# A new order of all steps in a fused attention and feed-forward kernel on one core

## The chip, the cores and the metric

The kernel runs on one core of one Trainium2 chip. The metric is the device time of one execution in microseconds (us). Engines are named as the profile names them: PE is TensorE, DVE is VectorE, ACT is ScalarE, POOL is GpSimd, and SP is the engine whose queue issues the DMAs.

## What is computed

Per batch and head, k and v (576 rows of 64) are averaged in groups of 8, which leaves 72 rows; softmax attention of the 576 queries against them gives x, and x goes through a layer norm and a feed-forward block with a residual:

```python
k_p = k.reshape(B, H, Sp, pool, D).mean(axis=3)
v_p = v.reshape(B, H, Sp, pool, D).mean(axis=3)
scores = scale * np.matmul(q, k_p.transpose(0, 1, 3, 2))
...
attn = attn / (np.sum(attn, axis=-1, keepdims=True) + 1e-09)
attn_out = np.matmul(attn, v_p)
...
xn = (x - mu) / np.sqrt(var + 1e-06) * g_ln
ch = np.maximum(xn @ w_ch1, 0.0) @ w_ch2
return x + ch
```

There are 8 batches, 8 heads, 512 model columns and 2048 hidden columns, all in float32.

## The kernel before

The 4608 tokens are 36 tiles of 128, taken in 9 chunks of 512. Weights and activations are held as pairs of float16 numbers (a high and a low part), so that a float32 product is three float16 products on PE. From chunk 2 on the products with w1 (L779, step U), and from chunk 3 on those with w2 (L1002, step E), use a scheme with seven products in place of eight, for which sums of weight blocks are formed (steps T and F) and those for w2 are kept in DRAM and streamed back (L977, step D). Chunks 0 and 1 take the direct way: L1067 for w1 (step I) and L1102 for w2 (steps O and P).

At the start everything has to be made ready. The weights are loaded raw (R, L326) and put together in several pieces (C: ACT L337 and L358, POOL L343, DVE L349). The largest element of each weight sets a power of two for the split. For that (M1 for w1, M2 for w2) DVE takes a maximum per partition (L365, L366, L272, L273), PE copies it across (L295) and DVE reduces it again (L304). Only then can S split the weight: ACT writes the high part (L309), DVE the low part (L311). In the same time the first batches of k and v are averaged on PE (K L1218, V L1234), later ones on DVE (L1132, L1156). Step A makes the scores of a tile (L490, later L482), the exponentials (L504, L513, L522) and the transposed weights, by PE for tiles 0 to 4 (L527), later by a transposing DMA (L552, tile pt). Step B multiplies them with the values (L587 for tiles 0 to 4, L589 and L590 later), divides (L597, L605, L607, L615), takes mean and variance (L620 to L624), normalizes (L629) and transposes the result for the feed-forward (L640, L642, L644). The later form of B needs the pooled v as float16 pairs va and vb; the last piece of step V makes them with four small DMAs (L424, L425), and each batch does so once.

Nothing in the program chooses an order when it runs. START (L57 to L200) is a string of 2433 tokens, each naming a step with its arguments. A step is a generator, and every token runs it on to its next `yield`:

```python
def step(token):
    if token not in begun:
        name, *args = token.split(".")
        begun[token] = iter(ops[name](*map(int, args)) or ())
    next(begun[token], None)

with tc.manual_schedule():
    for token in START.split():
        step(token)
```

Each engine carries out its instructions in the order in which the tokens issued them, and waits at an instruction until what it needs is there. All DMAs named above go through SP's one queue, so a DMA that waits holds up those behind it. Below, V.1 is the step V of batch 1, B.5 the step B of tile 5, and M1.0 the second half-step of w1's maximum.

Of the kernel before, what the change touches and what calls it, by code (L numbers as in the profile page):

```python
# [62 lines left out]
C.1.5.1 C.1.5.1 V.1 M1.0 B.3 K.1 A.4 B.0 B.2 C.1.5.1 S.1.0 R.2.6 C.2.6.1 C.2.6.1 B.3 S.1.0 B.3 B.3 HV.2.0 R.1.6
C.2.6.1 S.1.1 C.2.6.1 B.0 C.2.0.1.1 V.1 S.1.1 C.1.6.1 A.4 HK.2.0 B.1 HK.2.0 B.2 S.1.2 B.1 A.4 C.2.0.1.1 A.5 A.5 B.1
HK.2.1 S.1.2 A.4 HK.2.1 R.2.2 B.2 S.1.3 A.4 B.1 C.2.0.1.1 B.3 S.1.3 I.0.1.0 I.0.0.0 A.4 B.2 C.1.6.1 I.0.1.0 B.3
C.1.6.1 I.0.0.0 I.0.0.0 I.0.1.0 A.5 A.5 C.1.6.1 I.0.0.0 I.0.0.0 I.0.0.0 C.2.2.1.1 C.2.2.1.1 R.2.3 R.2.7 I.0.0.0
C.2.3.1 B.4 M1.1 M1.1 A.5 C.2.2.1.1 HV.2.0 I.0.0.1 I.0.0.1 M1.1 V.1 I.0.0.1 B.4 I.0.0.1 A.6 I.0.0.0 A.5 I.0.0.0
I.0.0.0 C.2.2.1.1 HK.2.0 HK.2.0 S.1.4 S.1.4 C.2.3.1 I.0.1.1 C.2.7.1 I.0.1.1 I.0.1.1 C.2.3.1 I.0.1.0 I.0.0.0 I.0.0.0
C.2.7.1 I.0.0.1 A.6 S.1.5 S.1.5 I.0.1.0 HV.2.0 I.0.1.0 I.0.1.1 I.0.0.1 I.0.1.0 C.2.3.1 R.2.4 C.2.4.1 C.2.4.1 A.6 V.1
V.1 I.0.1.1 I.0.1.1 A.5 R.2.5 I.0.0.1 B.4 C.2.4.1 S.1.6 I.0.1.0 HV.2.0 S.1.6 I.0.0.1 I.0.0.1 A.6 V.1 C.2.4.1 I.0.0.1  # L70
A.7 I.0.0.1 C.2.7.1 S.1.7 S.1.7 I.0.1.1 I.0.1.1 C.2.5.1.1 I.0.2 C.2.5.1.1 I.0.0.1 C.2.7.1 HV.2.0 R.2.1 I.0.1.1 V.1
I.0.2 V.1 HV.2.0 C.2.1.1 I.0.3 HK.2.1 C.2.1.1 I.0.1.0 A.6 I.0.2 QS.10 A.6 C.2.1.1 A.7 C.2.1.1 QS.9 C.2.5.1.1 T.0.0.1
I.0.1.0 I.0.2 I.0.1.0 HV.2.0 I.0.1.1 X.0 HV.2.0 I.0.1.0 I.0.2 I.0.1.1 B.4 T.0.0.1 I.0.2 I.0.2 A.8 C.2.5.1.1 A.7 QS.9
I.0.2 I.0.3 I.0.1.1 T.0.0.1 A.6 B.5 A.7 M2 I.0.2 I.0.2 I.0.2 M2 M2 QS.9 I.0.3 I.0.3 S.2.0 I.0.3 S.2.0 S.2.1 HK.2.1
I.0.0.1 HV.3.1 I.0.2 S.2.1 Y.0 I.0.3 HV.3.1 I.0.3 I.0.3 S.2.2 S.2.2 B.4 QS.9 S.2.3 X.1 Y.1 X.2 HV.3.1 T.0.0.1 I.0.3
B.5 I.0.3 S.2.3 I.0.3 KS.2 A.7 A.7 HV.3.1 B.5 I.0.3 O.0.0 A.8 QS.9 B.6 KS.2 HV.3.1 S.2.4 O.0.0 O.0.0 HV.3.1 HK.3.0
KS.2 KS.2 T.0.0.1 X.3 HV.3.1 Y.3 A.8 A.8 S.2.4 B.7 QS.10 A.8 KS.2 B.7 O.0.0 O.0.0 S.2.5 HV.3.1 QS.10 S.2.5 HV.2.1 B.5
B.4 QS.10 QS.10 B.7 B.5 S.2.6 O.0.0 KS.2 O.0.0 Y.2 HV.2.1 HV.2.1 B.6 B.6 S.2.6 B.5 HV.2.1 N.0.1 S.2.7 S.2.7 O.0.1 QS.9
B.6 B.5 HK.3.0 A.9 A.8 HV.2.1 QS.10 T.0.0.1 O.0.1 B.7 T.0.0.1 B.6 O.0.1 T.0.0.1 O.0.1 T.1.0.1 O.0.1 HV.2.1 QS.11 B.6
B.6 HK.3.0 T.0.0.1 A.9 HV.2.1 QS.11 QS.11 QS.11 A.9 T.1.0.1 T.1.0.1 B.7 B.7 N.0.0 A.10 HV.2.1 O.0.1 QS.12 QS.11 QS.11  # L80
B.4 T.1.0.1 B.7 A.9 HV.2.1 O.0.0 HK.3.0 HK.3.1 QS.12 O.0.1 T.0.0.1 HV.3.0 O.0.1 N.0.2 O.0.1 B.8 T.0.0.1 B.8 O.0.1 B.4
O.0.1 T.0.0.1 HK.3.1 A.9 O.0.1 I.1.2 HV.2.1 I.1.1 QS.12 A.10 HV.3.0 HK.3.1 A.10 HK.3.1 I.1.2 T.0.0.1 HV.2.1 HV.2.1
I.1.2 I.1.1 I.1.1 T.1.0.1 I.1.3 T.1.0.1 B.8 I.1.0 HV.2.1 A.9 T.1.0.1 HV.3.0 HV.3.0 HV.2.1 KS.3 HV.3.0 T.0.1.1 QS.12
QS.12 I.1.3 B.8 I.1.1 A.10 A.11 A.11 I.1.0 I.1.0 I.1.0 I.1.1 I.1.1 KS.3 KS.3 T.1.0.1 I.1.0 B.9 HV.3.0 A.10 A.11 I.1.0
QS.12 T.0.1.1 QS.13 T.1.0.1 B.9 KS.3 QS.13 T.1.0.1 B.9 I.1.3 I.1.0 A.10 A.11 B.8 I.1.2 I.1.2 I.1.0 KS.3 A.11 A.12
HV.4.1 B.10 A.12 B.10 HV.4.1 I.1.2 I.1.3 T.1.0.1 B.9 A.11 I.1.3 QS.13 QS.14 I.1.2 I.1.0 I.1.0 HK.4.0 A.12 B.11 KS.3
QS.13 B.8 I.1.0 I.1.3 HK.4.0 B.9 B.9 T.0.1.1 I.1.0 B.10 B.8 HV.3.0 HV.3.0 QS.13 A.12 B.9 B.9 B.11 B.9 I.1.1 HV.4.1
I.1.3 I.1.3 I.1.1 I.1.1 A.12 I.1.3 B.11 B.11 I.1.1 I.1.1 I.1.2 QS.13 I.1.1 B.9 B.9 HV.4.1 HV.4.1 I.1.3 I.1.2 I.1.2
T.0.1.1 O.1.0 T.0.1.1 A.13 T.1.0.1 B.10 QS.14 F.0.0.0 T.1.0.1 F.0.0.0 T.1.1 B.9 B.9 I.1.3 F.0.0.0 I.1.2 I.1.2 F.0.0.0
A.12 QS.15 B.10 B.10 F.0.0.0 F.0.0.0 I.1.3 HK.4.0 HV.4.1 QS.14 F.0.0.0 T.1.1 B.11 O.1.0 F.0.0.0 QS.14 QS.14 B.11 B.11  # L90
O.1.1 QS.14 B.11 B.11 B.11 B.11 B.11 A.13 F.0.0.0 QS.15 F.0.0.0 QS.15 O.1.0 O.1.0 QS.15 HV.4.1 N.1.3 F.0.0.0 B.11
T.1.1 O.1.0 HV.4.1 O.1.0 O.1.1 O.1.0 U.2.1.5 F.0.1.1 F.0.1.1 A.14 B.10 HV.3.1 HV.3.1 T.1.1 F.0.0.0 O.1.0 U.2.1.6 T.1.1
U.2.1.5 U.2.1.1 U.2.1.3 HV.3.1 HV.3.1 HV.4.0 A.13 U.2.1.1 F.0.1.1 U.2.1.6 HV.3.1 U.2.0.1 B.12 U.2.1.2 U.2.1.6 HK.4.0
A.13 F.0.1.1 QS.15 F.1.0.1 U.2.1.3 U.2.1.3 U.2.1.3 QS.16 HV.3.1 HK.4.1 U.2.0.1 U.2.1.7 U.2.1.7 HV.4.0 A.14 U.2.0.2
U.2.1.4 QS.15 F.1.0.1 HV.4.0 A.13 O.1.1 F.1.0.1 U.2.0.2 U.2.1.7 U.2.1.7 HK.4.1 F.1.0.1 F.1.0.1 F.1.0.1 HV.4.0 HV.4.0
U.2.0.2 B.12 U.2.1.2 U.2.1.2 B.12 A.14 U.2.1.4 U.2.1.4 F.1.0.1 A.13 HV.4.0 HV.4.0 N.1.1 F.1.0.1 O.1.1 A.15 A.15
U.2.0.6 U.2.0.6 O.1.1 F.1.0.1 F.1.0.1 O.1.1 O.1.1 F.1.0.1 QS.16 F.1.1.0 QS.16 HV.4.0 U.2.0.5 QS.17 F.1.0.1 F.1.1.0
# [1233 lines left out]
```

## Time and profile before

| | |
|---|---|
| time, median of 3 runs | 808.04 us (807.31 to 808.33) |
| the profiled execution | 807.27 us, of which the span is 805.6 us |
| PE busy | 97% of the span |
| DVE busy | 84% |
| ACT busy | 61% |
| POOL busy | 38% |
| mean granted clock | 0.985 |

The share of a clock is of 2.4 GHz. A row of a timeline or of the waits says what an engine did and, in brackets, how long it was idle before that and which engine's instruction, line and tile ended the idle time. A wait is therefore put down to the instruction that came last.

### The profile page before, as it was taken

How to read it: one execution, taken by the hardware profiler on the slowest of the kernel's cores; microseconds unless marked ns; L12 is line 12 of the kernel's file. 1: busy time of each engine (PE TensorE's matmuls, PEld its weight loads, DVE VectorE, ACT ScalarE, POOL GpSimd, SP SyncE). 2: the span in 40 equal slices, each digit the busy share in tenths (PEclk: the TensorE clock that was granted, in tenths of full speed). 3: DMA queues.
4: the chain of work that ended last, by engine and by line, in shares of the span. 5: the costliest groups of instructions: out<-in, count | busy, mean ns of one | idle time of the engine just before them, and what ended most of it. 6: DMA issues, size and time to landing. Idle time of an engine off the chain costs nothing.

```text
span 805.6 us, 17573 instructions
## 1 busy us (share of the span) xinstructions
PE 781.4 (97%) x6800; PEld 610.4 (76%) x6800; DVE 675.2 (84%) x1549; ACT 489.1 (61%) x935; POOL 306.1 (38%) x270
## 2 busy tenths in 40 slices
...
GB/s 336 385 159 227 282 254 238 190 153 129 94 176 157 169 132 173 190 245 139 204 180 149 132 175 180 151 161 164 191 109 159 119 152 145 105 126 111 54 53 131
DMA packets 240068, 136.52 MB, mean 169 GB/s; under 512 B 157952, under 2 KB 217328, under 8 KB 236912
## 3 DMA queue, kind: packets, MB, share of 16 engines
...
q10 hardware_dynamic: 144, 0.13, 0.0%
...
## 4 chain that ended last, share of the span: by engine, by line
PE 78%; DVE 11%; DMA 5%; ACT 4%; issue 1%; POOL 0%; SPq 0%; DVEq 0%; ACTq 0%
PE ps_f L779 30%; PE ps_f L1002 24%; PE ps_f L1102 10%; PE ps_f L1067 6%; DMA vr<-in_v_dram 2%; DVE w L311 2%; PE ps L482 1%; PE ps_f L1218 1%; PE ps L589 1%; PE ps_f L1234 1%; PE ps L590 1%; PE ps L587 1%; DMA kr<-in_kT_dram 1%; DMA w<-in_kn_dram 1%; DVE vp L1156 1%
## 5 line engine op out<-in xcount | busy, mean ns | idle before, releaser
L1002 PE MATMUL ps_f<-w,ring 128*128 128x256 f16 x2016 | 229.9, 273 | 1.4 <-DVE vb L415 0.9
L1002 PEld LDWEIGHTS <-ring 128*128 128x128 f16 x2016 | 196.3, 98 | 25.1 <-DMA w<-d2T 1.8
L779 PE MATMUL ps_f<-zz,w 128*128 128x256 f16 x1344 | 160.0, 273 | 0.7 <-DVE ring L837 0.7
L779 PEld LDWEIGHTS <-w 128*128 128x128 f16 x1344 | 130.0, 98 | 16.2 <-DVE ring L837 1.0
L1102 PE MATMUL ps_f<-w,ring 128*128 128x512 f16 x576 | 127.6, 379 | 2.4 <-DVE w L311 2.3
L779 PE MATMUL ps_f<-zz,raw 128*128 128x256 f16 x1008 | 121.5, 273 | 0.0
L831 POOL TENSOR_TENSOR ring<-v,ring 128x512 f16<-128x512 f32 x48 | 57.0, 1191 | 154.0 <-ACT ring L828 135.7
L1102 PEld LDWEIGHTS <-ring 128*128 128x128 f16 x576 | 55.7, 98 | 67.9 <-issue 3.0
L779 PEld LDWEIGHTS <-raw 128*128 128x128 f16 x1008 | 97.6, 98 | 11.7
L1067 PE MATMUL ps_f<-zz,w 128*128 128x512 f16 (+1 forms) x480 | 85.2, 336 | 0.7 <-DVE w L311 0.7
L1067 PEld LDWEIGHTS <-w 128*128 128x128 f16 x480 | 46.3, 98 | 35.6 <-DVE w L311 1.2
L541 POOL TENSOR_TENSOR phl<-e,phl 128x512 f16<-128x512 f32 x31 | 36.7, 1185 | 77.4 <-ACT phl L533 68.0
L687 POOL TENSOR_TENSOR hl<-z,hl 128x512 f16<-128x512 f32 x28 | 34.6, 1246 | 66.6 <-ACT hl L685 58.4
L831 POOL TENSOR_TENSOR ring<-ring 128x512 f16<-128x512 f32 x24 | 28.7, 1197 | 49.4 <-ACT ring L828 37.8
L629 ACT ACTIVATE z<-x,nb,y 128x512 f32<-128x512 f32 x36 | 29.2, 812 | 29.0 <-DVE nb L624 27.7
L504 DVE TENSOR_REDUCE mx<-ps 128x8 f32<-128x576 f32 x36 | 27.0, 750 | 11.9 <-PE ps L490 8.5
L615 ACT ACTIVATE x<-ps,rs 128x64 f32<-128x64 f32 x144 | 33.4, 315 | 5.2 <-DVE x L607 4.0
L1156 DVE TENSOR_REDUCE vp<-vr 72x64 f32<-72x512 f32 x48 | 32.4, 674 | 3.1 <-DMA vr<-in_v_dram 3.0
L828 ACT CAST ring<-v 128x512 f16<-128x512 f32 x48 | 29.8, 621 | 8.3 <-DVE v L837 6.4
L533 ACT CAST phl<-e 128x1024 f16<-128x1024 f32 x31 | 32.5, 1047 | 2.0 <-DMA pt<-phl 1.0
L343 POOL TENSOR_SCALAR raw<-raw 128x1024 int32<-128x1024 uint16 x12 | 14.5, 1208 | 48.9 <-DMA raw<-in_w_dram 39.7
L569 DVE TENSOR_SCALAR a<-y,ve 128x1 f32<-128x1 f32 x108 | 29.5, 273 | 3.9
...
## 6 DMA issues: line engine op xcount, KB each, us to landing
...
```

Of the source, the lines that this page charges most:

```text
L533: nc.scalar.copy(out=ph[:, :, :, 0:KA], in_=e[:, :, 0:KA].unsqueeze(1).broadcast_to([P, 2, H, KA]))
L541: nc.gpsimd.tensor_tensor(out=ph[:, 0, :, KA:P], in0=e[:, :, 0:KA], in1=ph[:, 0, :, 0:KA], op=ALU.subtract)
L569: nc.vector.tensor_scalar(out=a, in0=y, scalar1=ve, scalar2=y, op0=ALU.mult, op1=ALU.mult)
L615: nc.scalar.activation(out=xh[:, 4 + i, :], in_=px[:, 1, i, 0:D], func=AF.Copy, scale=rs[:, 4 + i : 5 + i])
L687: nc.gpsimd.tensor_tensor(out=hl[:, 1, r], in0=part, in1=hl[:, 0, r], op=ALU.subtract)
L779: nc.tensor.matmul(ps[:, j], lhsT=w_form(wb, int(m == 2), k)[:, fs], rhs=z_form(za, int(m == 1), k), start=(first and i == 0 and j == 0), ...
L828: nc.scalar.copy(out=hi, in_=src)
L831: eng.tensor_tensor(out=lo, in0=src, in1=hi, op=ALU.subtract)
L1002: nc.tensor.matmul(parts[i], lhsT=h[:, hp, f, i * P : (i + 1) * P], rhs=w[:, f // FPB, wp, f % FPB], start=(first and f == k == 0 and (i = ...
L1067: nc.tensor.matmul(ps, lhsT=w[:, part, fs], rhs=zT[:, kz, cols], start=(n == 0), stop=(n == 3 * NKT - 1),)
L1102: nc.tensor.matmul(ps, lhsT=h[:, part, i, cols], rhs=w[:, wp, j], start=(n == 0), stop=(n == 3 * NFT // 2 - 1),)
L1156: nc.vector.tensor_reduce(out=vp[b][:, h, 0:D], in_=vraw.pop((b, h)), axis=AX.X, op=ALU.add,)
```

## The change

Only the string START differs: 148 lines of tokens are replaced. The tokens are the same steps in another order, so each engine gets the same instructions (13128 on PE with its weight loads, 1551 on DVE, 895 on ACT, 275 on POOL, 387 on SP), and buffers have the same number and size; which buffer of a set a step gets follows its place. The order was searched for away from the chip, by replays in which each transfer lands late by a random amount. One line of the 148, the one around the second half of w1's maximum:

```diff
-C.1.2.1 B.1 A.3 B.3 V.1 B.0 V.1 C.1.4.1 B.2 C.1.4.1 C.1.1.0.1 C.2.0.1.1 K.1 K.1 B.2 V.1 C.1.5.1 B.3 M1.0 A.4 M1.0
+B.1 G B.0 R.2.0 LV.1 A.3 C.2.0.1.1 A.3 B.0 M1.0 C.1.4.1 B.2 M1.0 M1.0 V.1 B.3 R.1.5 C.1.5.1 B.1 K.1 A.4 B.2 V.1 R.2.6
```

PE, from the transposes of a tile of the first batch to the first scores of batch 1. L295 with `rowmax` is w1's maximum on its way across the partitions; L1234 and L1218 average v and k of batch 1, L587 and L640 are steps B of tiles 2 to 4. Before:

```order
L1234 MATMUL ps_f<-zz,kp_all 72x512
L587 MATMUL ps_400<-vp,pt 128x65 x8
L1234 MATMUL ps_f<-zz,kp_all 72x512
L640 MATMUL ps_f<-ident_101,z 128x128 x4
L1234 MATMUL ps_f<-zz,kp_all 72x512
L1218 MATMUL ps_f<-kp_all,w_88 128x16 x4
L1218 MATMUL ps_f<-kp_all,w_88 128x8 x4
L1234 MATMUL ps_f<-zz,kp_all 72x512
L295 LDWEIGHTS rowmax
L295 MATMUL ps_f<-ident,rowmax 128x128
L1234 MATMUL ps_f<-kr,kp_all 72x512
```

After:

```order
L640 MATMUL ps_f<-ident_101,z 128x128 x4
L295 LDWEIGHTS rowmax
L295 MATMUL ps_f<-ident,rowmax 128x128
L1234 MATMUL ps_f<-zz,kp_all 72x512
L587 MATMUL ps_446<-vp,pt 128x65 x8
L1218 MATMUL ps_f<-kp_all,w_88 128x16 x4
L1234 MATMUL ps_f<-zz,kp_all 72x512 x2
L1218 MATMUL ps_f<-kp_all,w_88 128x8 x4
L1234 MATMUL ps_f<-zz,kp_all 72x512
L1234 MATMUL ps_f<-kr,kp_all 72x512
L640 MATMUL ps_f<-ident_101,z 128x128 x4
L490 MATMUL ps_521<-kblk_103,q 64x144
```

The maximum moved from behind most of batch 1's averaging to ahead of all of it. The product of the values (L587) and all averages now stand behind it, and the first scores of batch 1 (L490), which stood directly behind the averages, have one more group of transposes (L640) ahead of them.

DVE, around the last splits of w2 (`w_88<-w_88,ws`, L311); L1113 adds a finished product of w2 to x and so frees its bank, L1156 averages v. Before, with the last two splits:

```order
L463 SCALAR_TENSOR_TENSOR q<-q,s_1368 128x8x64
L1113 SCALAR_TENSOR_TENSOR x<-ps_f,c_out,x 128x512
L1156 TENSOR_REDUCE vp<-vr 72x64
L597 TENSOR_SCALAR sm<-ps_1279,cv 128x8
L605 RECIPROCAL rs<-sm 128x8
L607 TENSOR_TENSOR x<-ps_1279,rs 128x256
L311 SCALAR_TENSOR_TENSOR w_88<-w_88,ws 128x1024
L1156 TENSOR_REDUCE vp<-vr 72x64
L311 SCALAR_TENSOR_TENSOR w_88<-w_88,ws 128x1024
```

After, with the third but last and the last but one:

```order
L463 SCALAR_TENSOR_TENSOR q<-q,s_1221 128x8x64
L311 SCALAR_TENSOR_TENSOR w_88<-w_88,ws 128x1024
L1156 TENSOR_REDUCE vp<-vr 72x64
L311 SCALAR_TENSOR_TENSOR w_88<-w_88,ws 128x1024
L1113 SCALAR_TENSOR_TENSOR x<-ps_f,c_out,x 128x512
L597 TENSOR_SCALAR sm<-ps_1382,cv 128x8
L605 RECIPROCAL rs<-sm 128x8
L607 TENSOR_TENSOR x<-ps_1382,rs 128x256
```

and the last one, 18 rows further down:

```order
L624 TENSOR_SCALAR nb<-mv_1410,y 128x1
L1148 SCALAR_TENSOR_TENSOR kblk_103<-kp_all,sv,kblk_103 64x4x72 x2
L311 SCALAR_TENSOR_TENSOR w_88<-w_88,ws 128x1024
L1132 TENSOR_REDUCE kp_all<-kr 128x72
L620 BN_STATS st<-x 128x6
```

The splits are further apart, and the last but one has moved from behind to ahead of the division of a tile (L597 to L607).

SP, around the four copies that make va and vb of batch 1 (L424, L425). L1259 and L1263 put a buffer of hidden values away and fetch it back, L326 is a raw weight load, L552 a transposing DMA of an attention tile. Before:

```order
L401 DMA vr<-in_v_dram 72x512
L326 DMA raw<-in_w_dram 128x2048
L424 DMA va<-vh 64x520
L425 DMA vb<-vh 8x520
L424 DMA va<-vh 64x520
L425 DMA vb<-vh 8x520
L397 DMA kr<-in_kT_dram 128x576
L449 DMA q<-in_qn_dram 128x512 x2
L401 DMA vr<-in_v_dram 72x512
L1259 DMA hd_1044<-ring 128x4096
```

After:

```order
L1259 DMA hd_1018<-ring 128x4096
L1263 DMA ring<-hd_946 128x4096
L552 DMA_TRANSPOSE pt<-phl_105 128x16x128
L401 DMA vr<-in_v_dram 72x512
L449 DMA q<-in_qn_dram 128x512
L424 DMA va<-vh 64x520
L425 DMA vb<-vh 8x520
L424 DMA va<-vh 64x520
L425 DMA vb<-vh 8x520
L1263 DMA ring<-hd_1018 128x4096
```

The copies moved from directly behind the last raw load to behind the next transpose and a load of q that is new in front of them.

## Rows read from the trace of the kernel before

**Rows 1.** Page, part 1: busy us, share of the span, instructions.
```profile
PE 781.4 (97%) x6800; PEld 610.4 (76%) x6800; DVE 675.2 (84%) x1549; ACT 489.1 (61%) x935; POOL 306.1 (38%) x270
```

**Rows 2.** Stretches: length, busy us by engine, granted clock, DMA share, GB/s.
```profile
19.10:39.60 20.50, 18.84 (x136) 15.29 (x135) 16.37 (x35) 15.74 (x26) 5.45 (x4) 1.00 1.03 387
39.60:49.80 10.20, 10.06 (x31) 6.01 (x29) 8.29 (x30) 8.21 (x19) 1.51 (x2) 0.50 0.51 191
...
53.20:66.90 13.70, 9.41 (x46) 7.38 (x45) 13.26 (x27) 13.29 (x18) 1.82 (x1) 0.50 0.59 214
67.00:87.00 20.00, 19.73 (x197) 17.69 (x195) 19.42 (x44) 18.52 (x35) 6.09 (x6) 1.00 0.82 248
...
200.00:804.00 604.00, 599.71 (x5656) 496.03 (x5654) 515.06 (x1182) 358.82 (x708) 222.81 (x205) 1.00 0.62 148
```

**Rows 3.** PE's waits, whole span: us in total, times, longest.
```profile
PE ps_f L640 <- ACT z L629: 4.3, 2, 2.8
PE ps_f L1102 <- DVE w L311: 2.3, 2, 1.5
PE ps_f L295 <- DVE ring L1081: 1.6, 1, 1.6
PE ps_f L1002 <- DVE vb L415: 0.9, 1, 0.9
...
PE ps_f L779 <- DVE ring L837: 0.7, 1, 0.7
...
PE ps L589 <- DMA pt<-phl: 0.4, 1, 0.4
PE ps_f L1002 <- DMA w<-d2T: 0.3, 1, 0.3
...
PE ps_f L1002 <- DMA w<-d2B: 0.2, 1, 0.2
```

**Rows 4.** Timeline of PE, 20 to 70: start, us, what, [idle before].
```profile
22.51 2.89 PE L1234 MATMUL ps_f<-w,kp_all 128*72 128x512 f32 x6
...
41.92 3.68 PE L587 MATMUL ps<-vp,pt 72*128 72x65 f32 x16
45.39 1.92 PE L1234 MATMUL ps_f<-zz,kp_all 128*72 128x512 f32 x2
...
52.53 0.22 PE L295 MATMUL ps_f<-ident,rowmax 128*128 128x128 bf16 x1
...
66.99 3.22 PE L1067 MATMUL ps_f<-zz,w 128*128 128x256 f16 x28
```

**Rows 5.** Timeline of VectorE, 46 to 68: maximum of w1, what follows.
```profile
47.40 0.15 DVE L273 TENSOR_SCALAR rowmax<-rowmax 128x1 int32<-128x1 int32 x1
...
52.79 0.29 DVE L304 TENSOR_REDUCE allmax<-ps_f 128x1 f32<-128x128 f32 x1 [4.06 <-PE ps_f L295]
```

**Rows 6.** Timeline of all engines, 134 to 148: the last w2 splits.
```profile
139.37 3.27 DVE L311 SCALAR_TENSOR_TENSOR w<-w,ws 128x1024 f16<-128x1024 f32 x1
139.41 2.14 POOL L726 TENSOR_TENSOR w<-w 128x1024 f32<-128x1024 f16 x1
```

**Rows 7.** Line L311, its forms: duration in ns (min/median/max), first and last start.
```profile
L311 DVE SCALAR_TENSOR_TENSOR w<-w,ws x8: 1276/1284/3265, 110.6 to 143.8; 128x1024 f16<-128x1024 f32 x8
```

**Rows 8.** Timeline of SP, 86 to 108 and 784 to 806: batch 1's copies, last load.
```profile
89.69 0.51 SPq L424 DMA_DIRECT2D va<-vh  x1
...
91.63 0.67 SPq L425 DMA_DIRECT2D vb<-vh  x1
...
795.24 0.52 SPq L977 DMA_DIRECT2D w<-d2T  x1
```

**Rows 9.** Timeline of PE, 98 to 110 and 784 to 806: first use, product groups.
```profile
104.78 0.19 PE L589 MATMUL ps<-va,pt 128*128 128x65 f16 x1
...
105.29 2.75 PE L1067 MATMUL ps_f<-zz,w 128*128 128x512 f16 x12
...
799.45 2.79 PE L1002 MATMUL ps_f<-w,ring 128*128 128x256 f16 x24 [0.35 <-DMA w<-d2T]
```

More of the change, by code (lines that the diff above doesn't have):

```diff
@@ L63 @@
[L63 to L97, printed above, removed]
@@ new lines @@
+U.2.3.2 HV.4.1 O.1.1 A.14 U.2.3.2 U.2.3.2 QS.16 U.2.2.2 HV.5.0 A.15 U.2.2.2 U.2.2.2 F.2.1.1 HV.5.0 B.13 F.2.1.1
+F.3.0.1 F.2.1.1 KS.4 QS.17 P.2.2.0 B.12 P.2.2.0 HV.4.1 U.2.0.3 U.2.3.6 U.2.3.6 HV.4.1 HV.5.0 A.15 F.3.0.1 F.3.0.1
+U.2.3.5 A.16 U.2.3.6 KS.4 B.14 HK.5.0 B.14 U.2.2.6 U.2.2.6 A.16 I.1.2 U.2.3.7 HV.4.1 U.2.3.5 U.2.3.7 U.2.3.3 KS.4
+U.2.2.5 U.2.2.6 F.3.0.1 U.2.3.4 B.12 KS.4 HK.5.0 U.2.3.7 B.14 A.15 QS.18 QS.18 U.2.2.5 U.2.3.7 QS.18 U.2.3.3 U.2.3.3
+U.2.3.4 N.1.0 HV.5.0 HV.5.0 B.13 F.3.0.1 B.12 B.12 U.2.2.7 A.15 QS.18 U.2.2.7 A.16 B.13 U.2.2.7 U.2.2.7 HK.5.1 B.13
@@ new lines @@
+U.5.1.2 B.24 A.25 U.5.0.7 QS.28 U.5.0.3 U.5.0.4 U.5.0.4 HK.7.0 U.5.1.6 A.27 HV.7.1 HV.7.1 HV.7.1 U.5.2.1 U.5.1.5
+U.5.0.4 U.5.1.5 B.25 U.5.1.7 U.5.0.3 A.26 QS.30 A.26 D.5.0.1 E.5.0.1 U.5.0.4 U.5.1.7 U.5.1.4 U.5.2.1 U.5.0.4 A.27
+U.5.0.4 QS.28 U.5.1.3 HK.7.1 U.5.0.4 U.5.0.4 U.5.2.2 A.27 U.5.1.7 U.5.1.4 QS.28 U.5.0.3 U.5.1.7 A.26 U.5.1.4 U.5.1.3
+QS.28 U.5.1.3 QS.28 U.5.1.4 U.5.1.4 U.5.1.4 U.5.1.4 U.5.2.6 HV.7.1 E.5.0.1 B.25 U.5.1.3 E.5.0.6 D.5.0.2 E.5.0.2
+U.5.2.2 U.5.2.6 B.25 B.26 U.5.1.3 U.5.1.3 A.27 U.5.2.6 HK.7.1 E.5.0.6 U.5.2.2 B.26 HV.7.1 HV.7.1 A.28 OUT.18 QS.29
```

237 lines of the change are left out of this document (131 added, 106 removed).

## The prediction

> **What bounds the kernel.** I read the page's busy times first. PE is busy 97% of the span and DVE 84% [rows 1], so there is little to win in all: the span less PE's busy time is 24 us, and a part of that is the first load, which no order removes. The stretches come next [rows 2]. From 200 us on PE is busy 599.71 of 604.00 us, and its waits there add up to about 2.5 us; that is the reserve of three quarters of the kernel. From 67 to 87 us PE has 19.73 of 20 us. The reserve lies ahead of that: from 53.20 to 66.90 us PE is busy 9.41 of 13.70 us, at half clock, while DVE is busy 13.26. DVE is the bound there, since the first product with w1 (L1067) needs both the splits of w1 and the normalized tiles, and both come through DVE.
>
> The waits of PE, by line [rows 3], then say where each lost microsecond is: 4.3 us for the normalized tile z in that stretch, 2.3 us for the splits of w2, 1.6 us for a maximum that stands behind a hidden value's low part, and about 2.5 us in five short waits of the dense part (0.9, 0.7, 0.4, 0.3, 0.2). The timelines [rows 4, 5] show the first of these as a chain: DVE has w1's maximum per partition at 47.40 + 0.15 us, PE takes it across only at 52.53 us since it stands behind the averages of batch 1, and DVE sits idle for 4.06 us until 52.79. Only then can the splits begin.
>
> **The change, term by term.** The number of instructions on each engine is the same, so every term is a wait that goes, moves or comes. The sum is made against the profiled execution (807.27 us), which is 0.77 us under the median of 808.04; I add the sum to the median.
>
> *The start.* The maximum now goes across PE ahead of batch 1's averages, and the statistics of a tile stand on DVE in the meantime. The 4.06 us of idle time [rows 5] are gone: −4.06. In return two new waits of DVE come. First, the division of tile 3 (L597) needs a product of the values that stands behind an average: one L1234 at half clock is 0.96 us (1.92 for two), eight L587 are 1.84 (3.68 for sixteen) [rows 4], together 2.80, against 0.29 us of reduction and three small scalings of 0.15 us or a little more [rows 5] that DVE still has in hand: +1.9. Second, the first scores of batch 1 (L490), which DVE reduced only late before, now stand on DVE close behind the splits, while on PE they are behind four more averages, eight small groups of K and one more set of transposes. An average is 0.48 us at full clock (2.89 for six) and 0.96 at half [rows 4]; four of them are 1.9 or 3.8. With the rest, and less the DVE work that stands ahead of the scores, I estimate +1.5 at full clock and +4.1 at half. The start therefore comes to between −0.7 and +1.9. I take +0.5: half clock was granted in the stretch before the first L1067 [rows 2], but part of the averages may fall in a full one. L1067 then begins near 67.5, against 66.99 [rows 4].
>
> On the clock the row shows this: it fell to half at 39.6 us, directly behind 20.5 us in which PE was busy 18.84 at full clock [rows 2]. The Trainium skill, page "TensorE: Matmul & The Clock Gate", Part 1 on the clock gate, states that the throttled clock is the default and that activity releases it. By that rule PE, which has its waits packed closer here, would keep full speed, and the start would be at its lower end, −0.7 in place of +0.5. The row speaks against it, since a busy stretch did not keep the clock up; it stands as a rival below.
>
> *The last splits of w2.* PE waits 2.3 us for them in two waits, the longest 1.5 [rows 3]. One of the two splits took 3.27 us where its kind takes 1.28 [rows 6, 7], and a POOL sum (L726, 2.14 us) ran through the same time: 1.99 us more. In the new order the last but one stands ahead of the division of a tile, and the last has the statistics of a tile ahead of it, so POOL and DVE meet in another place. If both waits go it is −2.3, if the collision only moves 0. I take −1.5, as the splits come earlier with regard to the products, while the collision itself may stay; its cover would then be the product groups of 2.75 us each [rows 9].
>
> *The copies of batch 1's values.* Before, the four copies were issued from 89.69 to 91.63 + 0.67 us [rows 8], and B.5 used them at 104.78 [rows 9], so they never counted. Now they stand on SP behind a transposing DMA that waits for POOL and a load of q that waits for PE, and V's last step has one product group of 2.75 us [rows 9] between itself and B.5. The issue alone is 2.6 us. For the landing the nearest row is the last load of w2, 512 KB, issued at 795.24 [rows 8], for which PE waited until 799.45 [rows 9]; 4.2 us is an upper bound for these much smaller copies. Without the queue running ahead of the tokens B.5 is late by up to 2.6 + 4.2 − 2.75 = 4.1 us; if SP gets there one product group sooner, by 1.3 at most, or not at all. I take +1.0, bounds 0 and +4.1. Behind B.5 on PE all products wait, so this would lie on the path in full.
>
> *The maximum at 181.78.* PE waits 1.6 us for a bank that DVE frees [rows 3]. It has other neighbours now: between −1.6 and 0, I take −0.8, half.
>
> *The dense part.* Of its 2.5 us, 0.9 are DMA waits (0.4, 0.3, 0.2) [rows 3]. In the new order the loads of w2 that had least PE work between issue and use have more (2.8 us where it was 1.6, by the order and 0.11 us a product, 24 in 2.79 us [rows 9]), and the last of them is issued ahead of a store instead of behind it: −0.7. The 1.6 us for DVE (0.9 and 0.7) are likely to fall elsewhere, half of them: −0.8. Against that every one of the 600 us of steps has been re-dealt, and new waits of the size seen can come: I add +0.3. The term is −1.2; its bounds are −2.5 (all go) and +1.5 (two new waits as large as the largest there, and nothing goes).
>
> The sum: 0.5 − 1.5 + 1.0 − 0.8 − 1.2 = −2.0 us. From 808.04 that is 806.0.
>
> **The rivals.**
> *The start gains in full.* The wait of 4.06 us goes and PE runs at 2.4 GHz up to L1067, so that DVE finds its operands. For it: DVE was busy at all other times there, so its work is 4 us shorter. Against it: the granted clock of the stretch before. Then the start is −3, the copies cost 0, and the rest is as above: −3 − 1.5 − 0.8 − 1.2 = −6.5 at best, about −5.5 with a wait of 1 us left: 802.5.
> *Nothing but a redistribution.* DVE is 97% busy from 53 to 87 us [rows 2], and a wait removed ahead of a bound engine is given back there; the waits of the dense part only change places. The sum of the terms is then within 1.6 us of nothing: 808.
> *Slower: batch 1's operands are late.* Its place is the stretch up to B.5. The averages run at 1.2 GHz ahead of the scores, +1.9, and the copies land behind the product that needs them, +2.5 (between the two bounds above); of the gains only the splits' −1.5 remain. That is +2.9: 811. It decides at the time of the first L1067: where it begins later than 67.5 us and B.5 shows a wait for va or vb, this is the case.
>
> **How the numbers follow.** About 0.2% (1.6 us) is what a measurement of this kernel can tell from no change. My forecast, −2.0 with its own range of −4 to 0, has a chance of 0.40, of which 0.28 lie beyond −1.6. The full gain has 0.14 (all faster), the redistribution 0.19 (all same), the slower case 0.27 (all slower). Faster is 0.28 + 0.14 = 0.42, same 0.12 + 0.19 = 0.31, slower 0.27. The range from 802.0 to 811.0 holds the forecast, the redistribution, most of the full gain and half of the slower case.
>
> **What would show it.** Right: the all-max matmul (L295) begins near 44 us, DVE's idle time ahead of L304 is under 1 us, and L1067 begins between 66.3 and 68.9; PE's waits for L311 fall under 1 us; PE shows a wait of up to 2 us for DMA at B.5; the dense part has under 1.5 us of waits. Wrong: L1067 before 65 us (the full gain), or PE waiting for va or vb by more than 2 us, or waits of more than 3 us in the dense part, by lines that had none before.

## The result, and the profile after

The changed kernel took 799.98 us (median; 799.02 to 801.61), the kernel before 808.18 beside it: a ratio of 0.9893 (95% interval 0.9861 to 0.9925), or 8.2 us less. A second comparison of the two, in the experiments, gave 798.84 against 808.16, ratio 0.9903 (0.9873 to 0.9933). The prediction was 806.0, with a range from 802.0 to 811.0, so the time lies below the range. Its sign was right; the size was four times too small. Ratios and their intervals are of fast runs alone, and can differ a little from the quotient of two medians; four single runs in a slower state (903 us in p_split, 2867 us in a_warm, two of the kernel before) are left out of them.

The profiled execution took 801.61 us with a span of 799.9, so it is the slowest of its kernel, and 5.7 us of span lie between the two traces, not 8.2. Those 5.7 us are placed first. PE's waits in the new kernel, as [rows 3] has them for the one before (us in total, times, longest):

```profile
PE ps_f L640 <- ACT z L629: 3.6, 1, 3.6
PE ps_f L779 <- ACT ps_f L854: 1.2, 2, 0.8
PE ps L527 <- ACT w L309: 1.2, 1, 1.2
PE ps_f L1002 <- DVE ring L824: 1.0, 1, 1.0
PE ps_f L1002 <- DMA w<-d2B: 0.7, 1, 0.7
...
PE ps L590 <- DVE ring L1081: 0.3, 1, 0.3
```

Of the kernel before, beside the 2.3 us at L1102 and the 1.6 us at L295 of [rows 3], these fell into the stretch from 67 to 200 us:

```profile
PE ps_f L1067 <- DVE w L311: 0.7, 1, 0.7
PE ps L589 <- DVE e L513: 0.5, 1, 0.5
PE ps L587 <- ACT ps L337: 0.3, 1, 0.3
```

None of the waits for L311 is left, nor that of L295, nor any wait for the exponentials at L589. From the first product with w1 to 200 us only the 0.3 us at L590 remain. In the stretches (length, busy us of PE, PEld, DVE, ACT and POOL, granted clock, DMA share, GB/s) it is as plain:

```profile
67.00:87.00 20.00, 20.00 (x193) 17.69 (x192) 18.36 (x46) 17.23 (x34) 6.67 (x6) 0.97 0.82 254
...
152.00:200.00 48.00, 47.72 (x291) 22.98 (x290) 42.59 (x115) 29.89 (x62) 36.36 (x24) 1.00 0.70 159
```

In the rows shown PE is idle for 0.28 us of 48 and else not at all; from 92 to 152 us, left out here, it is busy 60.00 of 60 us.

Every trace can be taken apart in the same four pieces: when PE begins with w1 (L1067), what PE then waits up to 200 us, what it waits behind that (waits over 0.06 us, summed from PE's rows), and the rest.

| us | span | L1067 begins | waits to 200 | waits behind | rest |
|---|---|---|---|---|---|
| before | 805.6 | 66.99 | 5.5 | 2.5 | 730.6 |
| after | 799.9 | 65.92 | 0.3 | 3.2 | 730.5 |

So 5.2 of the 5.7 us are waits between 67 and 200 us, 1.1 us are the start, and 0.7 us is lost again in the dense part. That is the profile's answer; what holds in all runs, the experiments had to tell, since single runs of the kernel before lie anywhere from 802.5 to 814 us.

### The profile page after: what moved, and what is told of

Read it like the earlier page. It is cut to its first block, busy times and chain, and to the rows that moved or that the text cites. A ratio compares the mean times of both kernels' runs of the same rounds, so it can differ in the third digit from the quotient of the medians.

```text
span 799.9 us, 17591 instructions
## 1 busy us (share of the span) xinstructions
PE 780.6 (98%) x6800; PEld 611.2 (76%) x6800; DVE 679.7 (85%) x1549; ACT 487.7 (61%) x935; POOL 302.9 (38%) x270
## 4 chain that ended last, share of the span: by engine, by line
PE 77%; DVE 12%; DMA 4%; issue 1%; ACT 1%; SPq 0%; DVEq 0%; ACTq 0%
PE ps_f L779 27%; PE ps_f L1002 25%; PE ps_f L1102 10%; PE ps_f L1067 8%; DMA vr<-in_v_dram 2%; PE ps L482 2%; DVE w L311 2%; PE ps L587 1%; DVE vp L1156 1%; PE ps L589 1%; PE ps L590 1%; DMA kr<-in_kT_dram 1%; DVE x L1017 1%; DMA w<-d2B 1%; DVE a L569 1%
## 5 line engine op out<-in xcount | busy, mean ns | idle before, releaser
L1102 PE MATMUL ps_f<-w,ring 128*128 128x512 f16 x576 | 126.5, 379 | 0.0
L1102 PEld LDWEIGHTS <-ring 128*128 128x128 f16 x576 | 55.8, 98 | 65.1
L1067 PE MATMUL ps_f<-zz,w 128*128 128x512 f16 (+1 forms) x480 | 86.2, 340 | 0.0
L541 POOL TENSOR_TENSOR phl<-e,phl 128x512 f16<-128x512 f32 x31 | 38.3, 1234 | 94.7 <-ACT phl L533 82.1
L1067 PEld LDWEIGHTS <-w 128*128 128x128 f16 x480 | 47.0, 99 | 35.0 <-issue 0.2
L1156 DVE TENSOR_REDUCE vp<-vr 72x64 f32<-72x512 f32 x48 | 32.3, 674 | 4.2 <-DMA vr<-in_v_dram 4.2
L828 ACT CAST ring<-ring 128x512 f16<-128x512 f32 x48 | 29.1, 618 | 3.9 <-PE ps_f L1002 3.9
```

The costliest lines, as they stand in the source:

```text
L541: nc.gpsimd.tensor_tensor(out=ph[:, 0, :, KA:P], in0=e[:, :, 0:KA], in1=ph[:, 0, :, 0:KA], op=ALU.subtract)
L828: nc.scalar.copy(out=hi, in_=src)
L1067: nc.tensor.matmul(ps, lhsT=w[:, part, fs], rhs=zT[:, kz, cols], start=(n == 0), stop=(n == 3 * NKT - 1),)
L1102: nc.tensor.matmul(ps, lhsT=h[:, part, i, cols], rhs=w[:, wp, j], start=(n == 0), stop=(n == 3 * NFT // 2 - 1),)
L1156: nc.vector.tensor_reduce(out=vp[b][:, h, 0:D], in_=vraw.pop((b, h)), axis=AX.X, op=ALU.add,)
```

## The experiments

### Which stretch holds the gain

Strings START were put together from both orders: a piece of one, then all tokens that are left in the order of the other (`taken` stands for the tokens already used). Three take one stretch alone from the new order, a fourth the first two. The forms of w2 are its sums of weight blocks.

```diff
 # h_start: new start
-START = old
+START = new[:160] + [t for t in old if t not in taken]
 # h_mid: new stretch from L1067 to the first forms of w2
+START = old[:161] + (new[:615] less taken) + (old less taken)
 # h_dense: new behind the first forms of w2
+START = old[:614] + (new less taken)
 # h_front: new start and stretch
+START = new[:615] + (old less taken)
```

**h_start.** 

> The new order up to the first product with w1 (160 tokens), all other tokens in the order of the kernel before. Theory A (each stretch has its own waits, and the parts add up): the start is worth 1 to 1.5 us, as L1067 begins at 65.9 in place of 67.0 us, and the waits of PE from 67 to 200 us, 5.5 us before, stay at 4 to 6 us: 806 to 807.5 us. Theory B (the waits from 67 to 200 us go because the new start brings DVE ahead): they shrink to under 2 us here too: 801 to 803 us.

**h_mid.** 

> The order of the kernel before up to the first product with w1, then the new order up to the first forms of w2 (about 230 us), then the old one again. Theory A: L1067 begins at 67 us as before, the waits of PE from 67 to 200 us fall from 5.5 to under 1 us, the dense part keeps its 2.5 us: 802.5 to 804 us. Theory B: without the new start DVE is behind here as well, and the waits stay above 3 us: 805 to 808 us.

**h_dense.** 

> The order of the kernel before up to the first forms of w2, then the new order to the end. The traces show 2.5 us of waits of PE from 200 us on before and 3.2 us in the new kernel. Theory A: the dense part is worth nothing or costs up to 1 us: 807.5 to 809 us. The prediction's step (the dense part gains 1.2 us) would give 806.5 to 807 us, with the waits there at about 1.3 us.

**h_front.** 

> The new order up to the first forms of w2 (start and the stretch to some 230 us), then the order of the kernel before. If the gain sits in the stretch from 67 to 200 us alone (PE's waits there 0.2 to 0.3 us in the new kernel and in the run with only that stretch new, 5.5 us before), this is as fast as the new kernel: 799 to 804 us, with waits of 2 to 4 us from 200 us on. If the new order of the dense part belongs to the gain, it is slower than 805 us.

**a_again.** 

> The new kernel unchanged, beside the others of this call. If its gain is that of the waits from 67 to 200 us (5.2 us) and the start adds nothing certain, the ratio to the kernel before is 0.989 to 0.994, PE's waits from 67 to 200 us are under 1 us again, and L1067 begins anywhere between 62 and 69 us with the clock that PE is granted.

Measured, with the pieces of each one's trace:

| | median, us | ratio to before (95%) | span | L1067 begins | waits to 200 | behind |
|---|---|---|---|---|---|---|
| h_start | 809.43 | 1.0001 (0.9969 to 1.0034) | 801.9 | 62.39 | 5.5 | 2.6 |
| h_mid | 804.26 | 0.9944 (0.9914 to 0.9973) | 803.4 | 69.06 | 0.2 | 3.9 |
| h_dense | 808.74 | 1.0003 (0.9969 to 1.0038) | 803.7 | 63.72 | 4.9 | 3.6 |
| h_front | 800.31 | 0.9884 (0.9827 to 0.9941) | 801.3 | 65.70 | 1.2 | 4.2 |
| a_again | 798.84 | 0.9903 (0.9873 to 0.9933) | 800.0 | 65.69 | 1.7 | 2.4 |

The new stretch alone removes the waits, with the old start ahead of it. In the window from its L1067 on to 200 us h_mid has one wait:

```profile
PE ps L590 <- DMA vb<-vh: 0.2, 1, 0.2
```

while h_start has the old ones back, for the same lines as [rows 3]:

```profile
PE ps_f L1102 <- DVE w L311: 2.2, 2, 1.5
PE ps L587 <- DVE e L513: 1.4, 1, 1.4
```

Theory A holds: the gain is in the stretch, not carried into it by the start. The new start alone and the new dense part alone cannot be told from no change. (In h_start theory A wanted 806 to 807.5; it came out at 809.4. In h_mid it wanted 802.5 to 804; it came out at 804.3, with 3.9 us of waits behind 200 us where 2.5 were expected.) h_front, with four runs and so a wide interval, shows that the new dense part is not needed for the gain.

The 5.2 us of the first two traces is one pair. a_again, the same kernel as after, was expected under 1 us up to 200 us and shows 1.7, of which 1.4 are two waits at L1067 for DVE's L1081. Over the traces in the table and the first two, the new order of the stretch has 0.2 to 1.7 us of waits (after, h_mid, h_front, a_again) and the old one 4.9 to 5.5 (before, h_start, h_dense): a gain of 3.2 to 5.3 us. The 0.7 us lost behind 200 us did not come again in a_again, with 2.4 us there against 2.5 before.

### What the start's length follows

L1067 begins at 66.99, 69.06 and 63.72 us in three traces whose first 161 tokens are the same (before, h_mid, h_dense). The stretch from 20 to 70 us of these three, in this order:

```profile
20.00:70.00 50.00, 43.91 (x254) 33.36 (x253) 40.68 (x95) 41.12 (x70) 11.73 (x9) 0.76 0.70 256
```

```profile
20.00:70.00 50.00, 42.80 (x236) 34.14 (x235) 39.95 (x92) 39.35 (x67) 10.86 (x8) 0.76 0.68 253
```

```profile
20.00:70.00 50.00, 40.58 (x273) 31.07 (x271) 44.61 (x99) 43.87 (x74) 10.71 (x9) 0.90 0.74 272
```

The granted clock there is 0.76, 0.76 and 0.90. With the same tokens the clock falls and rises at other times from trace to trace, and L1067 begins up to 5.3 us earlier or later. The runs say the same: over 104 runs of the kernel before that were taken beside the experiments, a straight line through time against mean granted clock falls by 0.60 us for each 0.001 of clock. That is a relation; it does not say how much of the time the clock causes, and at 0.76 the two traces still lie 2.1 us apart.

The single move that the prediction took for the start's main event was then made alone in the kernel before:

```diff
-... C.1.2.1 B.1 A.3 B.3 V.1 ... B.2 C.1.4.1 C.1.1.0.1 ... B.3 M1.0 A.4 M1.0 ... V.1 M1.0 ...
+... C.1.2.1 C.1.1.0.1 B.1 M1.0 A.3 B.3 M1.0 V.1 ... B.2 M1.0 C.1.4.1 ...
```

**p_max.** 

> The kernel before with the maximum of w1 (M1.0) taken across PE ahead of most averages of batch 1, by moving its three tokens and the last sum that it needs. DVE's wait of 4.06 us for it falls under 1 us. If DVE bounds the start, L1067 begins 3 to 4 us earlier at an equal clock: 804 to 805 us. If PE's clock in the start sets its length, L1067 begins within 1.5 us of where the kernel before has it at that clock (66.5 us at a mean granted clock of 0.76 from 20 to 70 us, 63.7 at 0.90): 806.5 to 809 us.

Measured: 809.88 us, ratio 1.0012 (0.9986 to 1.0038). Timeline of DVE, and then of PE (start, us, what, idle before):

```profile
43.78 0.15 DVE L273 TENSOR_SCALAR rowmax<-rowmax 128x1 int32<-128x1 int32 x1
...
49.78 0.29 DVE L304 TENSOR_REDUCE allmax<-ps_f 128x1 f32<-128x128 f32 x1 [4.21 <-PE ps_f L295]
```

```profile
61.31 1.65 PE L640 MATMUL ps_f<-ident,z 128*128 128x128 f32 x8 [3.97 <-ACT z L629]
65.64 1.12 PE L640 MATMUL ps_f<-ident,z 128*128 128x128 f32 x4 [2.68 <-ACT z L629]
...
69.37 1.89 PE L1067 MATMUL ps_f<-zz,w 128*128 128x256 f16 x13
```

The maximum per partition was there 3.6 us earlier than in [rows 5] and known 3.0 us earlier, yet DVE still waited 4.21 us for it, since PE had the small products ahead of it to do first, and PE later waited 6.6 us for z, against 4.3 in [rows 3]. L1067 began at 69.37 with a mean clock of 0.76, in a trace that can be set beside before's 66.99 and h_mid's 69.06 at that clock. The earlier maximum gave nothing. Neither of the two theories is met: DVE's idle time was to fall under 1 us and did not, and L1067 came 2.9 us later than the 66.5 that the second one had for this clock. DVE did other work first, too: its first split of w1 began at 59.57 us, against 56.63 before, behind a division and statistics that now stood after the maximum. So p_max does not tell whether DVE bounds the start.

Matmuls whose results nobody reads were put between the small products of the start of the new kernel:

```diff
-B.0 ... B.1 ... B.2 ... K.1 ... K.1 (third)
+B.0 W.0 ... B.1 W.1 ... B.2 W.2 ... K.1 W.3 ... K.1 W.4
```

**a_warm.** 

> The new kernel with ten idle matmuls of 512 columns (0.2 us each) put between the small products of the start, from about 28 to 42 us, where the clock falls although PE is busy; their results are not used. If those small products are why the clock falls, the mean granted clock from 20 to 70 us rises from 0.80 to over 0.9, L1067 begins 2 to 4 us earlier than 65.9 us, and the kernel is 1 to 3 us faster than the new one. If not, the start gets 2 us longer and the kernel 1 to 2 us slower.

Measured: 798.52 us, ratio 0.9882 (0.9850 to 0.9915), not to be told from the new kernel's 0.9903. From 20 to 70 us its trace shows:

```profile
20.00:70.00 50.00, 43.27 (x298) 33.45 (x297) 44.74 (x100) 42.30 (x74) 10.94 (x9) 0.93 0.81 286
```

The clock was 0.93 there, against 0.80 in the new kernel, and L1067 began at 63.91 us against 65.92 and 65.69. The mean clock of its runs was 0.9948 against 0.9907. The runs say that the clock rose; the trace alone would not, as h_start's, with the same start and no such matmuls, has 0.93 as well. What the clock gave and what the ten matmuls cost can't be told apart in the time.

### Are the waits removed by single moves?

The prediction priced the splits of w2 by their place. This was tried in the kernel before in four ways.

```diff
 # p_split: DVE's part of the last two splits (second S.2.6, S.2.7) earlier
-... S.2.6 O.0.0 KS.2 O.0.0 Y.2 HV.2.1 HV.2.1 B.6 B.6 S.2.6 B.5 HV.2.1 N.0.1 S.2.7 S.2.7 O.0.1 ...
+... S.2.6 S.2.6 S.2.7 O.0.0 KS.2 O.0.0 Y.2 HV.2.1 HV.2.1 B.6 B.6 B.5 S.2.7 HV.2.1 N.0.1 O.0.1 ...
 # p_split2: both parts, to where the new order has them with regard to O.0.0
+... S.2.5 S.2.6 HV.2.1 ... B.5 S.2.6 S.2.7 O.0.0 KS.2 S.2.7 O.0.0 ... N.0.1 O.0.1 QS.9 ...
 # p_split3: p_split2, and the transpose of a q tile ahead of v's reductions
+... O.0.0 Y.2 QS.9 HV.2.1 HV.2.1 B.6 B.6 B.5 HV.2.1 N.0.1 O.0.1 ...
 # p_w2: all of M2 and S.2 some 12 tokens earlier
```

**p_split.** 

> The kernel before with one change: the low parts of the last two splits of w2 (the last pieces of S.2.6 and S.2.7) come earlier on DVE, the one ahead of the statistics of a tile and the addition of a product, the other directly behind its division. If the two waits of PE for L311 (0.75 and 1.51 us) came from the place alone, both go: -2.3 us, 805.5 to 806.2 us. If the collision of DVE with POOL's L726 makes them, an L311 of over 2 us stands beside a POOL sum again and at least 0.7 us of wait stays: -0.5 to -1.5 us. If DVE is the bound there, the wait comes back at another line within 20 us: no change.

**p_split2.** 

> The kernel before with the last two splits of w2 moved in both parts (ACT's high part and DVE's low part), to where the new order has them with regard to the products with w2; the earlier try moved DVE's part alone. If their place is the cause, PE's waits for L311 go (2.3 us) and the sum from 67 to 200 us falls from 5.5 to 3 to 3.7 us: 805.5 to 806.5 us. If DVE is short of time as a whole, other lines wait instead and the sum stays above 4.5 us: no change.

**p_split3.** 

> The run before with the last two splits of w2 moved in both parts, and beside that one step more: the transposing DMA of a q tile (last piece of QS.9, L468) is issued ahead of two reductions of v and the loads behind them on SP, not behind. In the run without it PE waited 3.9 us for that tile, and the waits for L311 were gone. If the queue of SP is what gave the wait back, the wait for q goes as well, and PE's waits from 67 to 200 us fall to 1.5 to 3 us: -2 to -3 us at an equal clock. If DVE is short of time as a whole, another line waits for 2 us or more and the sum stays above 4.5 us.

**p_w2.** 

> The kernel before with the maximum of w2 (M2) and all pieces of the splits of w2 (S.2) some 12 tokens earlier, nothing else. Theory A (the work that DVE must do before the products with w2 comes too late as a chain: maximum, split on ACT, split on DVE): the last split ends 3 to 6 us earlier than 145.7 us, PE's waits for L311 go (2.3 us before) and no wait of like size takes their place: -2 to -3 us, 805 to 806 us, waits from 67 to 200 us at about 3 us. Theory B (DVE is short of time there as a whole, so what comes earlier pushes something else back): the waits for L311 go, others come for z, q or the exponentials, and the sum stays above 4.5 us: no change.

| | median, us | ratio to before (95%) | waits to 200, us | of these for L311 |
|---|---|---|---|---|
| p_split | 808.75 | 0.9997 (0.9964 to 1.0030) | 5.3 | 1.0 |
| p_split2 | 811.68 | 1.0058 (1.0024 to 1.0092) | 5.8 | 0.4 |
| p_split3 | 810.09 | 1.0021 (0.9998 to 1.0044) | 5.8 | 0.2 |
| p_w2 | 813.46 | 1.0032 (0.9995 to 1.0070) | 8.3 | 0.3 |

Each time the waits for L311 shrank from 3.0 us (2.3 at L1102 and 0.7 at L1067) to 1.0 or less, and each time the sum stayed or grew. p_split2 shows how. Timeline of all engines from 128 to 152 us:

```profile
135.29 0.74 DVE L463 SCALAR_TENSOR_TENSOR q<-q,s 128x512 f16<-128x512 f32 x1
...
138.45 2.98 DVE L311 SCALAR_TENSOR_TENSOR w<-w,ws 128x1024 f16<-128x1024 f32 x1 [0.56 <-ACT w L309]
...
141.35 0.67 DVE L1156 TENSOR_REDUCE vp<-vr 72x64 f32<-72x512 f32 x1
...
142.05 0.33 SPq L401 DMA_DIRECT2D vr<-in_v_dram  x1
...
142.86 1.44 SPq L468 DMA_TRANSPOSE q<-q  x1
...
147.14 0.69 PE L482 MATMUL ps<-kblk,q 128*128 128x72 f16 x16 [3.90 <-DMA q<-q]
```

The transposing DMA of a q tile (L468) could go from 136.03 us on, when L463 ends; in p_split3, below, it does go right behind L463 (137.39 + 0.74 us). Here it stands on SP behind a load of v (L401), the load waits for DVE to have read the buffer (L1156), and that stands on DVE behind the split, which ran for 2.98 us in place of 1.28 beside POOL's L726. So the transpose is issued at 142.86, and PE waits 3.90 us for q at 147.14. The new order leaves more room there; the same steps in its trace:

```profile
134.54 1.23 SPq L468 DMA_TRANSPOSE q<-q  x1
...
141.76 0.68 PE L482 MATMUL ps<-kblk,q 128*128 128x72 f16 x16
```

The transpose is issued 7.2 us ahead of its use. p_split3 moved the transpose of that one tile, and the wait went to the next:

```profile
138.16 1.25 SPq L468 DMA_TRANSPOSE q<-q  x1
...
145.00 0.68 PE L482 MATMUL ps<-kblk,q 128*128 128x72 f16 x16
...
146.48 3.56 SPq L552 DMA_TRANSPOSE pt<-phl  x1
147.00 0.68 DVE L1156 TENSOR_REDUCE vp<-vr 72x64 f32<-72x512 f32 x1 [2.05 <-DMA vr<-in_v_dram]
...
150.15 0.49 SPq L401 DMA_DIRECT2D vr<-in_v_dram  x1
...
150.73 1.23 SPq L468 DMA_TRANSPOSE q<-q  x1
...
154.37 0.69 PE L482 MATMUL ps<-kblk,q 128*128 128x72 f16 x16 [3.51 <-DMA q<-q]
```

The first q tile is now in time (L468 at 138.16, L482 at 145.00 without a wait). The next stands behind a load of v again (L401 at 150.15). The reduction that frees this load's buffer had waited 2.05 us for the load before it, but was done at 147.68; what held the load longer was SP's queue, with an attention tile's transposing DMA (L552) until 150.04. So p_split3's first theory falls, since the wait did not go but moved one tile on; the queue carries the delay again, and what makes L552 last 3.56 us there stays open. In p_w2 the delay comes out at yet other lines:

```profile
PE ps L589 <- DVE e L513: 3.1, 2, 2.6
PE ps_f L295 <- DVE rowmax L273: 1.8, 1, 1.8
```

What DVE does earlier for w2, it does later for the attention tiles.

The other way round, the place of the splits was undone in the new kernel:

```diff
-... S.2.6 O.0.0 ... S.2.7 HV.2.1 ... HV.2.1 S.2.7 O.0.0 B.6 B.7 T.1.0.1 HK.3.0 B.6 HV.2.0 QS.9 O.0.1 ...
+... O.0.0 ... HV.2.1 ... HV.2.1 O.0.0 S.2.6 B.6 B.7 T.1.0.1 HK.3.0 S.2.7 B.6 HV.2.0 QS.9 S.2.7 O.0.1 ...
```

**a_split.** 

> The new kernel with one part undone: the last pieces of the splits of w2 (low part of S.2.6, both parts of S.2.7) come as late with regard to the products with w2 (O.0.0, O.0.1) as in the kernel before. If their place is what removed the two waits for L311, PE waits 1.5 to 3 us for L311 again and the kernel is 1.5 to 3 us slower than the new one in its own waits. If DVE has time to spare there in the new order, the wait is under 0.7 us.

In this kernel two sums of weight blocks on POOL run ahead of the splits that they read, and so use what stood there before: its numbers are not the kernel's, and POOL does not wait there. The amount of work is the same. Measured: 803.67 us, ratio 0.9952 (0.9928 to 0.9976), against 798.84 for the new kernel in the same comparison; waits up to 200 us 5.1 us against 1.7. Timeline:

```profile
140.80 1.27 DVE L311 SCALAR_TENSOR_TENSOR w<-w,ws 128x1024 f16<-128x1024 f32 x1
...
142.13 2.29 PE L1102 MATMUL ps_f<-w,ring 128*128 128x512 f16 x5 [3.35 <-DVE w L311]
```

One wait for L311 makes up the difference of the waits. The time differs by more, 4.8 us; behind that wait the granted clock was 0.51 from 142 to 145 us (see the last section). So the early splits are needed for the whole gain, though 0.9952 is left without them, and they are not enough: in the old surroundings they bring none.

### Does the stretch come apart?

The stretch was cut at the first product with w2.

```diff
 # h_mid1: new from L1067 to the first O.0.0
+START = old[:161] + (new[:368] less taken) + (old less taken)
 # h_mid2: new from the first O.0.0 to the first forms of w2
+START = old[:354] + (new[:615] less taken) + (old less taken)
```

**h_mid1.** 

> The kernel before up to the first product with w1 and from the first product with w2 (about 118 us) on; the new order between the two. If the gain of the stretch is of many small moves, this takes the waits up to 128 us (1.6 us before) and leaves those behind it: 3 to 4 us from 67 to 200 us. If DVE's work up to 118 us decides about the later waits too, the sum is under 2 us.

**h_mid2.** 

> The kernel before up to the first product with w2 (about 118 us) and from the first forms of w2 (about 230 us) on; the new order between the two. If the gain is of many small moves, this leaves 0.7 to 1.6 us of waits up to 128 us and takes those behind it (3.9 us): the sum from 67 to 200 us is 1 to 2 us, -3 to -4 us at an equal clock. If DVE's work up to 118 us decides, the splits of w2 come late here too and the sum stays above 3.5 us.

h_mid1: 806.01 us, ratio 0.9980 (0.9956 to 1.0004), waits up to 200 us 4.1. h_mid2: 809.44 us, ratio 1.0020 (0.9997 to 1.0044), waits 5.4. The waits of PE, of h_mid1 and then of h_mid2, from 62 to 200 us:

```profile
PE ps_f L295 <- DVE ring L1081: 1.5, 1, 1.5
PE ps L589 <- ACT x L615: 1.2, 1, 1.2
PE ps_f L1102 <- DVE w L311: 1.0, 1, 1.0
```

```profile
PE ps_f L295 <- DVE rowmax L273: 4.5, 1, 4.5
...
PE ps_f L1067 <- DVE w L311: 0.6, 1, 0.6
```

In h_mid1 the waits ahead of the cut are gone but for 0.5 us, 1.2 us comes at the seam (L589), and 2.5 us of the 4.5 behind it remain. In h_mid2 the old waits ahead of the cut stand (0.6 at L1067 among them) and 4.5 us comes at the seam, where DVE had to make up for steps that the new order has earlier (it was busy 4.90 of 5.00 us from 114 to 119 us). Behind it there is no wait up to 200 us. So each half of the new order has few waits of its own, and each lost at the seam what it gained. That fits a gain of many small moves that hand over to each other; which of them count, beside the splits, is not shown. The expected sum for h_mid2 did not come, because of its seam.

### What the four copies cost

```diff
-V.1 HV.3.1 Y.1 HV.3.1 S.2.1 I.0.2 A.7 I.0.3 QS.9 S.2.2 I.0.3 I.0.3 QS.9 B.5
+HV.3.1 Y.1 HV.3.1 S.2.1 I.0.2 A.7 I.0.3 QS.9 S.2.2 I.0.3 I.0.3 QS.9 V.1 B.5
```

**a_late.** 

> The new kernel with the last step of batch 1's values (the four copies that make va and vb) directly ahead of the first product that uses them, one product group of 2.75 us later than in the new order. The prediction's bound was 2.6 us of issue and up to 4.2 us of landing: PE would wait 4 to 6.8 us at L589. If the copies land within 1.5 us: a wait of 2 to 4 us. If SP's queue runs well ahead of the tokens: under 1.5 us.

Its time, taken once, was 807.2 us. Timeline of a_late, and then of h_front, whose order is that of the new kernel here:

```profile
113.44 0.54 SPq L424 DMA_DIRECT2D va<-vh  x1
...
114.02 0.67 SPq L425 DMA_DIRECT2D vb<-vh  x1
...
115.53 0.24 PE L589 MATMUL ps<-va,pt 128*128 128x65 f16 x1 [3.56 <-DMA va<-vh]
```

```profile
109.62 0.67 SPq L425 DMA_DIRECT2D vb<-vh  x1
...
111.12 0.19 PE L589 MATMUL ps<-va,pt 128*128 128x65 f16 x1 [0.80 <-DMA va<-vh]
...
111.51 0.10 PEld L590 LDWEIGHTS <-pt 88*128 88x128 f16 x1 [0.32 <-DMA vb<-vh]
```

With the copies a product group later PE waits 3.6 us. The last issue of va ends at 113.98 us, and PE, which waits for va, goes on at 115.53, 1.55 us later; the prediction allowed 4.2 us for the landing. In the new order the copies come just in time: no wait in the two traces of the new kernel, 0.8 + 0.2 us in h_front's.

## Why the prediction was wrong, point by point

**The stretch from 67 to 200 us: right mechanisms, far too small.** It stands in three terms, −1.5 for the splits, −0.8 for L295 and +1.0 for the copies: −1.3 together. The first two traces show −5.2 (5.5 to 0.3), a_again −3.8 (to 1.7), and the runs of h_mid give some 4.5 us (0.9944 of 808.1, give or take 2.4). Of the 3.9 us between −1.3 and −5.2, 0.8 is the splits, of which I took two thirds only, 0.8 is L295, 1.0 the copies, which cost nothing in the trace of after, and the last 1.3 are waits at L1067, L587 and L589 that the sum did not hold at all, less the 0.3 left at L590. I had kept them at their old size without saying so. The step that failed is the pricing of each wait by its own neighbours, with half or two thirds of it taken. The single moves show that this pricing would have been wrong in the other direction as well: the early splits, worth −2.3 by it, gave nothing three times (p_split, p_split3, and p_split2, which was slower). In their place the runs show waits that hang together: one that was removed alone came back at another line, for q or for the exponentials. That one shortage of DVE, ACT and SP stands behind them all is argued from this and not shown. Nor do they go all together or not at all: without the early splits a_split keeps about half of the gain (0.9952), and h_mid1 has 4.1 us of waits in place of 5.5.

**The start: the bound was misread.** I called DVE the bound from its 13.26 busy us of 13.70 [rows 2], and built the term from DVE's waits. DVE in the trace of after:

```profile
48.40 0.28 DVE L304 TENSOR_REDUCE allmax<-ps_f 128x1 f32<-128x128 f32 x1
...
49.39 0.17 DVE L597 TENSOR_SCALAR sm<-ps 128x8 f32<-128x8 f32 x1 [0.25 <-PE ps L587]
```

The wait of 4.06 us went as forecast. The two that were to come in return, +1.9 and +1.5 to +4.1, did not: L597 waited 0.25 us, and DVE has no other wait up to L1067. By the prediction's own reckoning L1067 would have begun 3.8 us earlier; in this trace it began 1.1 us earlier, with waits of PE of 3.6 us for z and 1.2 us for ACT's part of a split (4.3 for z in [rows 3]). In h_start's trace, with the same start and a clock of 0.93, it began at 62.39, 4.6 us before the kernel before. So DVE's idle time alone does not tell when L1067 begins. What does stays open: DVE is busy for nearly all of that time in both kernels, two of its splits of w1 took 2.06 and 2.20 us here where none took over 1.28 before, and L1067 moves by 5 us with the same tokens, along with the clock. p_max, with the maximum 3 us forward, gained nothing. The value taken, +0.5, is not refuted by the runs (h_start: 1.0001, give or take 2.7 us), but one profile could not have carried a term to a tenth of a microsecond.

**The dense part: no gain, in the profiles or the runs.** −1.2 was taken; the two traces of the new kernel show +0.7 and −0.1, h_dense 1.0003. Of the 0.9 us of DMA waits that the term put down to the loads of w2, 0.4 is for an attention tile (pt, L589) [rows 3]; the loads had 0.5, so −0.7 could not come from them. Their longer leads saved nothing for certain: 0.7 + 0.2 us in after, 0.2 in a_again, and new waits for L824 and L854 came in both. This is what the +0.3 for re-dealt steps stood for, and it was too small.

**The copies: +1.0 was the wrong size, the place was right.** The copies do stand at the edge, as the two traces at 0 and 1.0 us show.

**The clock's part was left out.** The runs of the new kernel have a mean clock of 0.9907 against 0.9868, which by 0.60 us for 0.001 is 2.4 us; at an equal clock, by that line, they are 6.4 us faster. That would account for most of what the medians differ by more than the traces, whose clocks are nearly equal (0.985 and 0.986). In the traces of before, after and a_again the clock is below 1.00 between 20 and 70 us alone, but for the last 4 us of the two new ones, so it is in the start that it is lost. Which part of the order raises it stays open: h_start's runs have 0.9875, h_mid's 0.9863, h_dense's 0.9900 and the four of h_front 0.9935. Some 1.4 us at an equal clock (6.4 less h_mid's 5.0) are not placed either, but the line is rough: h_front, with start and stretch new, comes out at 3.6 by it, and h_dense at 1.9 slower than before.

**The rivals.** The full gain (802.5) comes nearest in time, but by a mechanism that the runs do not show: L1067 did not begin before 65 us in either trace of the new kernel, the granted clock from 20 to 70 us was 0.80 in both and not full, and the start alone brought nothing. The redistribution, with a chance of 0.19, describes rightly what single moves do and wrongly what the whole order does. The slower case did not occur: no wait for va or vb in the new kernel. And what a measurement can tell was put at 0.2%; with the spread of single runs the intervals here are 0.3%, which the range should have held.
